# Attention and two gated MLPs on one core: the second MLP's rows 256 to 1279 summed by adding transfers

## The chip, the cores and the metric

The kernel runs on one core of a Trainium2 chip. The metric is the device time of one execution, in microseconds (us). Several executions are timed and their median is given; one more execution is recorded by the hardware profiler.

The engines of the core work beside each other, each through its own list of instructions in order: TensorE (PE, with its weight loads as PEld), VectorE (DVE), ScalarE (ACT), GpSimd (POOL) and SyncE (SP). Transfers between DRAM and on-chip memory are issued from an engine's list and carried out by 16 DMA engines.

## What is computed

Windowed attention gives a matrix x of 2304 tokens by 512; a gated MLP with a sigmoid maps it to another 2304 by 512, and a second gated MLP without the sigmoid maps that to the result:

```python
x = _attn_ref(q, k, v)                    # 4 x 8 heads, window 64, as 2304 x 512
gate = 1.0 / (1.0 + np.exp(-(x @ moe_w_gate)))
x = gate * (x @ moe_w_val) @ moe_w_out    # 512 -> 1536 -> 512
a = x @ moe2_w_a
b = x @ moe2_w_b
return (a * b @ moe2_w_out).astype(np.float32)
```

The MLP weights arrive as 64-bit floats, two 32-bit words each; the kernel rebuilds a 32-bit value from them.

## The kernel before

**Tiling.** The 2304 tokens are nine blocks of 256. The hidden width of 1536 is twelve pieces of 128 (`fc` from 0 to 11, `NF = 12`). Every 32-bit product is made of three TensorE products: each operand is split into a rounded high part and the rest, and high*high, high*low and low*high are summed in PSUM. A tile with an `h` or `l` at its end of the name is such a part.

**Stages.** First come attention and the first MLP of blocks 0 to 4. Then comes the stage that the change is in: the second MLP of the same blocks. Blocks 1 to 4 (tokens 256 to 1279) are taken together as a two by two block product, with seven products instead of eight (`quad`, line 849 for its matmuls, tiles qa, qb, qc). Block 0 is fitted in between by an ordinary product (`hidden`, line 472, tiles gps and vps, and `projection`, line 525, tile acc). After that the last four blocks (tokens 1280 to 2303) go through both MLPs.

**The loop of the stage.** For each `fc` the loop makes the hidden values h of 128 features for the two groups of 512 tokens (tiles hh and hl for one group, h for the other). After every second `fc` (`PAIR = 2`) the output product of these two pieces is put on a list `rest`: 8 jobs, one for each 128 tokens. There are six such pairs, called pair 0 to pair 5 below. A job is one call of `bank_sum`: six matmuls into one PSUM bank (line 987, tile accq, 128 by 512), and then one instruction that empties it. In pair 0 ScalarE copies the bank into the result tile (line 989, tile resf). In pairs 1 to 5 VectorE adds the bank to the result tile (line 991). The result tiles are four of 128 by 2 by 512 that stay on chip through the stage. In pair 5 each job also sends its 128 rows to DRAM from SyncE (line 1122).

**What else runs there.** The weights of the second MLP are decoded in the same stretch, three matrices for each `fc`, up to two pieces ahead. VectorE does the larger part (lines 379 to 401, tiles wi, ex, wa, wb), ScalarE splits and copies (lines 373 to 398), GpSimd makes four sums of weight halves (line 422, tiles s), their low parts (line 430, tiles wq) and one low part (line 401, tile wo). SyncE loads the raw words (tiles st_a, st_b, st_o) and stores the decoded parts in DRAM (tiles ka, kb, ko, kq) for the last blocks. At the end of the stage VectorE and ScalarE also build the operands of the next stage (lines 797, 798 and 805, tiles op and t, from xq), and GpSimd the sums of its first weights (lines 450 and 453, from the loaded tile wf).

**What sets the order.** The program is written in one order, and a scheduler places the instructions on each engine by a simulated timeline. `fill` takes jobs from `rest` and places them between the steps of the next quad; a table `counts` says how many after which step. PSUM has two banks for accq and acc together (`ps_acc`), so the third bank's first matmul waits until the first bank is emptied. The result tiles come from a pool of five buffers (`accp`); the fifth holds block 0's result.

Of the kernel before, what the change touches and what calls it, by code (L numbers as in the profile page):

```python
# [10 lines left out]
F32 = mybir.dt.float32  # L11
# [4 lines left out]
ALU = mybir.AluOpType  # L16
# [5 lines left out]
def tile_window_attention_gated_mlps(ctx, tc, q, k, v, w1g, w1v, w1o, w2a, w2b, w2o, out):  # L22
    nc = tc.nc
# [3 lines left out]
    P = 128  # L27
    NP = H // 2
    NF = DFF // P
    G = 3  # L30
    N = 256
# [3 lines left out]
    W = 2 * N  # L35
# [947 lines left out]
    def bank_sum(dst, pairs, begin):  # L983

        ps = ps_acc.tile([P, W], F32, tag="acc", name="accq")[:, 0:dst.shape[-1]]
        for n, (a, b) in enumerate(pairs):
            nc.tensor.matmul(ps, lhsT=a, rhs=b, start=n == 0, stop=n == len(pairs) - 1)  # L987
        if begin:
            nc.scalar.activation(out=dst, in_=ps, func=AF.Copy)
        else:  # L990
            nc.vector.tensor_tensor(out=dst, in0=ps, in1=dst, op=ALU.add)  # L991
# [114 lines left out]
    def row_banks(res, hs, rows, begin, end):  # L1106


        banks = []
        for i in range(2 * NP):  # L1110
            j, sl = i // NP, slice(i % NP * P, (i % NP + 1) * P)
            cols = (slice(0, CH), slice(CH, W)) if end and rows[0] > N and i == 2 * NP - 1 else (slice(0, W),)
            r0 = rows[j] + i % NP * P
            for c in cols:
                pairs = [(h[j][a][:, sl], o[b][:, c]) for o, h in hs for a, b in ((0, 0), (0, 1), (1, 0))]
                banks.append((pairs, res[i // 2][:, i % 2, c], out[r0:r0 + P, c]))
        for pairs, d, to in banks:

            def job(d=d, p=pairs, b=begin, to=to):
                bank_sum(d, p, b)  # L1120
                if end:
                    nc.sync.dma_start(out=to, in_=d)

            rest.append(job)
        return banks

    x_ops = next(built)
    fill(len(rest))
    x_ops = next(built)
# [15 lines left out]
                    i, at, mybir.DependencyInfo(mybir.DependencyClass.NoSync, mybir.DependencyReason.DATA), reason="paced"  # L1145
                )

    hs, h0s, res = [], [], None
    seconds = (
        lambda: late["hs"].tile([P, 2, W], F32R, tag="hs", name="h1"),  # L1150
        lambda: wts.tile([P, 2, DM], F32R, tag="wa", name="h1"),
# [2 lines left out]
    for fc in range(NF):  # L1154
        alone = ALONE.get(fc, ())
        for i, f0 in enumerate(alone):
            need(NF + f0, NEVER)
            w = parts[NF + f0]
            h0s.append((w, hidden(1, w, x[1, (0,)])))
            fill(2)  # L1160
            if i == len(alone) - 1:
                rest.append(lambda a=(1, 0, h0s, fc == 0, False): projection(*a))
                h0s = []
        need(NF + fc, NEVER)
        if fc == NF - 1:
            eased = len(nc.cur_bb.bb.instructions)
        limit[0] = min(NW - 1, NF + fc + 2)
        if fc == 0:
            res = [accp.tile([P, 2, W], F32, tag="xacc", name=f"resf{i}") for i in range(4)]
        w = parts[NF + fc]  # L1170
        g = [tmp.tile([P, W], F32, tag="hr", name=f"g{i}") for i in range(2)]
        counts = ((0, 0, 1, 1, 1, 1, 0), (0, 0, 1, 1, 1, 1, 0)) if len(rest) <= 4 else ((0, 1, 1, 1, 1, 1, 1), (0, 1, 1, 1, 1, 1, 1))
        extra = max(0, len(rest) - sum(counts[0]))

        def between(i):
            fill(counts[0][i] + (extra if i == 4 else 0))
            for _ in range(((0, 0, 0, 0, 2, 2, 2) if fc == 0 else (1, 1, 1, 0, 1, 1, 1))[i]):
                paced()

        hs.append((w["o"], quad(1, w, x_ops, between, g, seconds[fc % 3], lambda: None)))  # L1180
        if len(hs) == PAIR:
            fill(len(rest))
            row_banks(res, hs, (3 * N, N), fc == PAIR - 1, fc == NF - 1)
            hs = []
    late.clear()
    middle.close()
# [156 lines left out]
```

## Time and profile before

| what | us |
|---|---|
| median of three timed executions | 953.04 |
| lowest and highest of them | 951.15, 953.58 |
| the profiled execution, its own time | 955.45 |
| the profiled execution, span from first to last instruction | 953.5 |
| PE busy within the span | 925.9 |
| DVE, ACT, POOL busy | 708.4, 478.8, 303.3 |

The profiled execution took 955.45 us, of which the span is 953.5; the other 1.95 us lie around it. All times inside the trace count from the start of the span. "Busy" of PE is modelled from pipelined matmuls: six matmuls of 512 columns that wait for nothing follow each other in 1.36 us.

An engine's idle time is put down to the instruction that released it. PE is busy for 97% of the span, so its idle stretches, with their releasers, are where an edit that leaves its matmuls alone can act. The stage of the change lasts from about 375 to 582 us.

### The profile page before, as it was taken

The page shows a single profiled execution, that of the slowest core. Times are in us where ns is not written, and L with a number is a line of the kernel's source. Part 1 is how long each engine was busy: PE and PEld are TensorE (multiplying, and loading weights), DVE is VectorE, ACT ScalarE, POOL GpSimd, SP SyncE. Part 2 cuts the span into 40 slices and gives each one's busy share as a digit, 9 for nine tenths or more (in the row PEclk, how much of TensorE's full clock was granted, in tenths as well). Part 3 has the DMA queues.
Part 4 walks back from the last instruction along what each step waited for, and adds up shares of the span by engine and source line. Part 5 has one row for each costly group of instructions (what it writes and reads, how often), then busy time and mean ns, then how long its engine had stood idle before and what let it go on. Part 6 is the DMA issues. An engine that isn't in the chain of part 4 may idle for free.

```text
span 953.5 us, 15652 instructions
## 1 busy us (share of the span) xinstructions
PE 925.9 (97%) x5504; PEld 773.1 (81%) x5504; DVE 708.4 (74%) x1379; ACT 478.8 (50%) x1063; POOL 303.3 (32%) x321
## 2 busy tenths in 40 slices
PE   7899999999999999999999989999999999999998
PEld 6698888887887788778877777788888888888886
DVE  6998787786569799788999875778788773354445
ACT  7897555686744456564555534655444243211111
POOL 4543222343226714362655336544430000000000
PEclk9999999999999999999999999999999999999999
DMA  8987598988568626565877566354547675554212
GB/s 203 237 237 221 197 326 291 336 286 245 153 220 310 225 109 220 195 220 178 269 236 261 210 198 222 111 188 158 158 150 220 198 275 153 159 173 134 89 66 88
DMA packets 144685, 193.69 MB, mean 203 GB/s; under 512 B 63584, under 2 KB 98912, under 8 KB 143968
## 3 DMA queue, kind: packets, MB, share of 16 engines
q1 hardware_dynamic: 144608, 192.71, 62.5%
q8 instruction: 43, 0.70, 0.3%
q14 instruction: 34, 0.28, 0.1%
HBM read 118.75 MB, written 69.47 MB: 197 GB/s over the span
## 4 chain that ended last, share of the span: by engine, by line
PE 69%; DVE 14%; DMA 5%; POOL 4%; ACT 4%; issue 3%; SPq 0%; DVEq 0%; POOLq 0%; ACTq 0%
PE qa L849 16%; PE accq L987 11%; PE qb L849 8%; PE gps L472 7%; PE vps L472 6%; PE accm L573 6%; PE qc L849 4%; PE accy L950 3%; PE accx L950 2%; DVE ex L392 2%; DVE wi L382 2%; PE xps L228 2%; DVE wi L379 1%; DVE wi L386 1%; DMA st_o<-in_moe_w_out_dram 1%
## 5 line engine op out<-in xcount | busy, mean ns | idle before, releaser
L849 PE MATMUL qa<-op,wq 128*128 128x512 f32 x432 | 112.9, 391 | 2.7 <-ACT r L868 2.3
L849 PE MATMUL qb<-op,wq 128*128 128x512 f32 x432 | 110.7, 390 | 0.9 <-POOL wq L430 0.6
L868 ACT ACTIVATE r<-qa 128x512 f32<-128x512 f32 x108 | 62.5, 594 | 90.0 <-PE qa L849 88.8
L472 PE MATMUL vps<-xh,wb 128*128 128x256 f32 (+1 forms) x392 | 105.6, 338 | 0.2 <-ACT hr L496 0.2
L472 PE MATMUL gps<-xh,wa 128*128 128x256 f32 (+1 forms) x392 | 105.2, 338 | 0.0
L849 PEld LDWEIGHTS qa<-op,wq 128*128 128x128 f32 x432 | 80.9, 188 | 20.4 <-ACT r L868 3.0
L849 PEld LDWEIGHTS qb<-op,wq 128*128 128x128 f32 x432 | 81.0, 188 | 18.4 <-POOL wq L430 1.0
L573 PE MATMUL accm<-hh,wo 128*128 128x512 f32 (+1 forms) x296 | 85.6, 357 | 1.6 <-DVE gacc L550 1.3
L386 POOL TENSOR_TENSOR wi<-wi,low 128x512 int32<-128x512 int32 x36 | 50.1, 1393 | 113.2 <-DVE wi L382 78.3
L472 PEld LDWEIGHTS gps<-xh,wa 128*128 128x128 f32 x392 | 69.2, 191 | 8.5 <-DVE hl L483 0.3
L472 PEld LDWEIGHTS vps<-xh,wb 128*128 128x128 f32 x392 | 69.0, 190 | 8.0 <-ACT hr L496 0.4
L987 PE MATMUL accq<-wo,h 128*128 128x512 f32 (+1 forms) x300 | 71.2, 382 | 3.8 <-DVE resf L991 3.7
L987 PEld LDWEIGHTS accq<-wo,h 128*128 128x128 f32 x300 | 54.8, 188 | 15.8 <-DVE resf L991 4.7
L472 PE MATMUL gps<-xl,wa 128*128 128x256 f32 (+1 forms) x196 | 65.9, 336 | 0.5 <-DVE xl L237 0.5
L472 PE MATMUL vps<-xl,wb 128*128 128x256 f32 (+1 forms) x196 | 65.7, 335 | 0.0
L392 DVE SCALAR_TENSOR_TENSOR ex<-ex,wi 128x512 f32<-128x512 f32 x72 | 53.3, 741 | 14.6 <-ACT ex L376 7.4
L481 ACT ACTIVATE hh<-qa 128x512 fp32r<-128x512 f32 x36 | 21.5, 597 | 84.4 <-DVE qa L881 55.5
L573 PEld LDWEIGHTS accm<-hh,wo 128*128 128x128 f32 x296 | 52.9, 189 | 11.9 <-DVE gacc L550 4.0
L987 PE MATMUL accq<-wo,hh 128*128 128x512 f32 x184 | 56.3, 397 | 1.5 <-ACT hh L481 1.4
L849 PE MATMUL qa<-op,wb 128*128 128x512 f32 x216 | 55.2, 391 | 1.9 <-ACT r L868 1.9
L849 PE MATMUL qc<-op,wa 128*128 128x512 f32 x216 | 56.9, 390 | 0.0
L189 ACT ACTIVATE pr<-pr,stat 128x128 f32<-128x128 f32 x144 | 54.0, 391 | 5.4 <-DVE stat L183 5.2
(180 smaller groups left out, 2154.9 us busy)
## 6 DMA issues: line engine op xcount, KB each, us to landing
wo<-ko SPq DMA_DIRECT2D x27, 512.0 KB, 4.2
wa<-ka SPq DMA_DIRECT2D x27, 512.0 KB, 4.4
st_o<-in_moe_w_out_dram SPq DMA_DIRECT2D x24, 512.0 KB, 5.0
ka<-wa SPq DMA_DIRECT2D x24, 512.0 KB, 5.4
kb<-wb SPq DMA_DIRECT2D x24, 512.0 KB, 3.9
ko<-wo SPq DMA_DIRECT2D x24, 512.0 KB, 5.1
kq<-wq SPq DMA_DIRECT2D x48, 256.0 KB, 4.5
wq<-kq SPq DMA_DIRECT2D x48, 256.0 KB, 3.2
```

The lines of the kernel that those rows point to most:

```text
L189: nc.scalar.activation(out=pr[e][:, j, :], in_=pr[e][:, j, :], func=AF.Exp, bias=nmax[:, e, j:j + 1], scale=-1.0, accum_out=None if t in O ...
L228: nc.tensor.matmul(xps[dims, j, rows], lhsT=vv[:, 2 * j + e, :], rhs=pt[e][:, j, rows], start=True, stop=True)
L382: nc.vector.scalar_tensor_tensor(out=wi, in0=w1, scalar=-(1 << 30), in1=wi, op0=ALU.bitwise_and, op1=ALU.bitwise_or)
L386: (nc.vector if F >= NF else nc.gpsimd).tensor_tensor(out=wi, in0=wi, in1=low, op=ALU.add)
L392: nc.vector.scalar_tensor_tensor(out=wf, in0=wf, scalar=SMALLEST, in1=wi.bitcast(F32), op0=ALU.is_ge, op1=ALU.mult)
L472: nc.tensor.matmul(ps, lhsT=a[:, c * P:(c + 1) * P], rhs=b[:, c, :], start=(n == 0), stop=(n == 3 * NP - 1))
L481: nc.scalar.activation(out=hh, in_=hr, func=AF.Copy, scale=factor)
L573: nc.tensor.matmul(ps[:, m], lhsT=a[:, sl], rhs=b, start=k == 0, stop=k == total - 1)
L849: nc.tensor.matmul(ps, lhsT=a[:, c * P:(c + 1) * P], rhs=b[:, c, :], start=first and n == 0, stop=n == 5, skip_group_check=True,)
L868: nc.scalar.activation(out=r[n], in_=ps, func=AF.Copy)
L950: nc.tensor.matmul(bank[k], lhsT=a[n][i][:, sl], rhs=b[n][j], start=start and m == 0, stop=m == 2, skip_group_check=True,)
L987: nc.tensor.matmul(ps, lhsT=a, rhs=b, start=n == 0, stop=n == len(pairs) - 1)
```

## The change

In the stage of tokens 256 to 1279, every pair's banks are now emptied by ScalarE copies, into tiles called `added` of 128 by 2 by 512 that hold two banks (256 rows) each. A tile is sent to the result in DRAM when both halves are filled: pair 0 by plain stores from SyncE, pairs 1 to 5 by transfers issued from GpSimd that add to what lies in DRAM (`accum_op`). The four result tiles that stayed on chip, and the stores at the end of pair 5, are gone. A tile's send is written two jobs after its second bank (`unsent`), so a pair has nine entries on `rest` instead of eight; the ninth only sends. The manual dependency in `send` keeps the scheduler from placing a transfer ahead of the matmul written before it.

So 40 VectorE adds of a bank become 40 ScalarE copies (48 copies in all, 8 of them were there), and 9 stores of 256 or 128 KB become 4 plain stores and 20 adding transfers of 512 KB. The matmuls stay the same in kind and number.

```diff
+    def added_rows(hs, rows, begin):
+        for i in range(2 * NP):
+            j, sl = i // NP, slice(i % NP * P, (i % NP + 1) * P)
+            pairs = [(h[j][a][:, sl], o[b]) for o, h in hs for a, b in ((0, 0), (0, 1), (1, 0))]
+            r0 = rows[j] + (i % NP - 1) * P
+
+            def job(i=i, p=pairs, to=out[r0:r0 + 2 * P].rearrange("(a p) f -> p a f", p=P) if i % 2 else None):
+                if i % 2 == 0:
+                    added[0] = accp.tile([P, 2, W], F32, tag="xacc", name="added")
+                bank_sum(added[0][:, i % 2], p, True)
+                if i % 2 == 0 and unsent:
+                    unsent.pop()()
+                if i % 2:
+                    unsent.append(lambda t=added[0]: send(t, to, begin))
+
+            rest.append(job)
+        rest.append(lambda: unsent.pop()())
+
+    unsent = []
+
+    def send(t, to, begin):
+        if begin:
+            nc.sync.dma_start(out=to, in_=t)
+        else:
+            at = next(i.name for i in reversed(nc.cur_bb.bb.instructions) if i.engine == mybir.EngineType.PE)
+            since = len(nc.cur_bb.bb.instructions)
+            nc.gpsimd.dma_start(out=to, in_=t, accum_op=ALU.add)
+            for i in nc.cur_bb.bb.instructions[since:]:
+                tc.add_manual_dep(
+                    i, at, mybir.DependencyInfo(mybir.DependencyClass.NoSync, mybir.DependencyReason.DATA), reason="send"
+                )
...
-        if fc == 0:
-            res = [accp.tile([P, 2, W], F32, tag="xacc", name=f"resf{i}") for i in range(4)]
...
-            row_banks(res, hs, (3 * N, N), fc == PAIR - 1, fc == NF - 1)
+            added_rows(hs, (3 * N, N), fc == PAIR - 1)
```

How this moves the instructions is shown at three places at the end of the stage, where pair 5 is emptied. Names are those of the section on the kernel before; a number after a name is a buffer's, and the same tile has another number in the two kernels.

VectorE, before: the adds of pair 5 stand between the steps that build the next stage's operands.

```order
L805 TENSOR_TENSOR t_6901<-xq_6822,t_6863 128x1024
L991 TENSOR_TENSOR resf_4826<-accq,resf_4826 128x512 x2
L798 TENSOR_TENSOR op_6903<-t_6901,op_6903 128x1024
L498 TENSOR_TENSOR vps<-vps,hr 128x256
L991 TENSOR_TENSOR resf_4827<-accq,resf_4827 128x512
L483 SCALAR_TENSOR_TENSOR hl<-vps,hh 128x256
L805 TENSOR_TENSOR t_6939<-xq_6822,xq_6820 128x1024
L991 TENSOR_TENSOR resf_4827<-accq,resf_4827 128x512
L991 TENSOR_TENSOR resf_4828<-accq,resf_4828 128x512
L798 TENSOR_TENSOR op_6941<-t_6939,op_6941 128x1024
```

VectorE, after, the same place:

```order
L805 TENSOR_TENSOR t_6937<-xq_6858,t_6899 128x1024
L798 TENSOR_TENSOR op_6939<-t_6937,op_6939 128x1024
L498 TENSOR_TENSOR vps<-vps,hr 128x256
L483 SCALAR_TENSOR_TENSOR hl<-vps,hh 128x256
L805 TENSOR_TENSOR t_6975<-xq_6858,xq_6856 128x1024
L597 TENSOR_TENSOR xacc_4866<-acc_7088,xacc_4866 128x512
L798 TENSOR_TENSOR op_6977<-t_6975,op_6977 128x1024
```

The adds are gone from VectorE, and the add of block 0's bank (line 597) has moved ahead of the last operand but one.

ScalarE, before, at the same place (line 452 copies the high part of a weight sum, line 797 that of an operand):

```order
L481 ACTIVATE hh<-vps 128x256
L797 ACTIVATE op_6903<-t_6901 128x1024
L452 ACTIVATE wq_7093<-s_7091 128x256
L481 ACTIVATE hh<-vps 128x256
L452 ACTIVATE wq_7098<-s_7096 128x256
L452 ACTIVATE wq_7103<-s_7101 128x256
L797 ACTIVATE op_6941<-t_6939 128x1024
```

ScalarE, after, the same place:

```order
L989 ACTIVATE added<-accq 128x512
L481 ACTIVATE hh<-vps 128x256
L989 ACTIVATE added<-accq 128x512 x2
L797 ACTIVATE op_6939<-t_6937 128x1024
L452 ACTIVATE wq_7120<-s_7118 128x256
L452 ACTIVATE wq_7125<-s_7123 128x256
L989 ACTIVATE added<-accq 128x512
L452 ACTIVATE wq_7130<-s_7128 128x256
L989 ACTIVATE added<-accq 128x512
L481 ACTIVATE hh<-vps 128x256
L797 ACTIVATE op_6977<-t_6975 128x1024
```

The copies of pair 5's last five banks now stand between the weight and the operand copies of the next stage.

GpSimd, after, from the last decoded matrix to the second group of weight sums of the next stage:

```order
L401 TENSOR_TENSOR wo<-ex,wo 128x512
L1155 DMA out_dram<-added 128x2x512 x5
L450 TENSOR_TENSOR s_6988<-wf 128x256
L450 TENSOR_TENSOR s_6993<-s_6988,wf 128x256
L450 TENSOR_TENSOR s_6998<-wf 128x256
L453 TENSOR_TENSOR wq_6990<-s_6988,wq_6990 128x256
L453 TENSOR_TENSOR wq_6995<-s_6993,wq_6995 128x256
L453 TENSOR_TENSOR wq_7000<-s_6998,wq_7000 128x256
L450 TENSOR_TENSOR s_7003<-wf,s_6993 128x256
L453 TENSOR_TENSOR wq_7005<-s_7003,wq_7005 128x256
L1155 DMA out_dram<-added 128x2x512
L450 TENSOR_TENSOR s_7118<-wf 128x256
```

Before, line 450 followed line 401 directly; now the four transfers of pair 4 and the first of pair 5 stand between them, and the other three of pair 5 between the sums. The first twelve, of pairs 1 to 3, stand among lines 422, 430 and 401 in the same way, two for each `fc`.

## Rows read from the trace of the kernel before

**Rows 1.** The page: busy us, share of the span and instructions of each engine.

```profile
PE 925.9 (97%) x5504; PEld 773.1 (81%) x5504; DVE 708.4 (74%) x1379; ACT 478.8 (50%) x1063; POOL 303.3 (32%) x321
```

**Rows 2.** Stretches: length, busy us (instructions) by engine, granted clock, DMA share, GB/s.

```profile
375.00:430.00 55.00, 51.79 (x248) 43.05 (x247) 44.84 (x66) 33.31 (x66) 26.53 (x27) 0.97 0.64 228
430.00:540.00 110.00, 107.98 (x488) 88.29 (x488) 104.88 (x163) 60.35 (x117) 54.08 (x56) 1.00 0.69 231
540.00:582.00 42.00, 37.73 (x202) 31.86 (x201) 31.89 (x43) 14.24 (x25) 14.86 (x16) 1.00 0.55 192
```

**Rows 3.** PE in order of time: start, length, [idle before, its releaser].

```profile
483.09 1.61 PE L849 MATMUL qa<-op,wa 128*128 128x512 f32 x6 [0.58 <-DVE g L871]
...
515.21 0.70 PE L849 MATMUL qb<-op,wq 128*128 128x512 f32 x2 [0.30 <-DVE hl L483]
...
528.27 1.19 PE L987 MATMUL accq<-wo,hh 128*128 128x512 f32 x4 [0.57 <-ACT hh L481]
533.67 1.21 PE L849 MATMUL qb<-op,wq 128*128 128x512 f32 x4 [0.58 <-POOL wq L430]
...
569.85 4.41 PE L987 MATMUL accq<-wo,h 128*128 128x512 f32 x18 [2.48 <-DVE resf L991]
575.45 1.70 PE L987 MATMUL accq<-wo,h 128*128 128x256 f32 x12 [1.20 <-DVE resf L991]
577.55 0.73 PE L525 MATMUL acc<-wo,hh 128*128 128x512 f32 x2 [0.40 <-DVE resf L991]
```

**Rows 4.** DVE by group from 430 to 580: busy, mean ns, idle before.

```profile
L991 DVE TENSOR_TENSOR resf<-accq,resf 128x512 f32<-128x512 f32 (+1 forms) x41 | 26.7, 667 | 2.1 <-PE accq L987 2.0
```

**Rows 5.** Line 989: ns min/median/max, starts; the last list has no entry.

```profile
L989 ACT ACTIVATE resf<-accq x8: 579/598/599, 393.7 to 414.5; 128x512 f32<-128x512 f32 x8
...
who waited for it (us, times):
```

**Rows 6.** DVE in order of time, inside pair 3 and pair 5.

```profile
523.90 0.68 DVE L991 TENSOR_TENSOR resf<-accq,resf 128x512 f32<-128x512 f32 x1
...
569.12 1.27 DVE L991 TENSOR_TENSOR resf<-accq,resf 128x512 f32<-128x512 f32 x2
570.39 1.22 DVE L798 TENSOR_TENSOR op<-t,op 128x1024 fp32r<-128x1024 f32 x1
```

**Rows 7.** ACT by group from 430 to 580: busy, mean ns, idle before, releaser.

```profile
L452 ACT ACTIVATE wq<-s 128x256 fp32r<-128x256 f32 x8 | 3.3, 416 | 12.4 <-POOL s L450 12.2
```

**Rows 8.** ACT in order of time: an operand's high part, and a staged matrix read.

```profile
454.53 0.68 ACT L376 ACTIVATE ex<-st_b 128x512 f32<-128x512 f32 x1 [1.41 <-POOL wo L401]
...
569.23 1.06 ACT L797 ACTIVATE op<-t 128x1024 fp32r<-128x1024 f32 x1 [1.77 <-DVE t L805]
```

**Rows 9.** POOL: line 430 by duration, line 422 by group, and one row in time.

```profile
L430 POOL TENSOR_TENSOR wq<-s,wq x48: 732/1177/1270, 293.8 to 536.6; 128x256 fp32r<-128x256 f32 x48
...
L422 POOL TENSOR_TENSOR s<-ex 128x256 f32<-128x256 f32 x12 | 10.1, 844 | 41.0 <-DVE ex L392 41.0
...
561.41 0.73 POOL L450 TENSOR_TENSOR s<-wf 128x256 f32<-128x256 f32 x1 [21.47 <-DMA wf<-kf]
```

**Rows 10.** Transfers from 430 to 580: count, KB each, median us to landing; one issue on SP.

```profile
ko<-wo SPq DMA_DIRECT2D x7, 512.0 KB, 4.0
ka<-wa SPq DMA_DIRECT2D x6, 512.0 KB, 4.9
...
441.10 0.38 SPq L353 DMA_DIRECT2D st_b<-in_moe_w_b_dram  x1
```

**Rows 11.** DVE in order of time: first and last result tile, pair 4, then pair 5.

```profile
535.29 1.28 DVE L991 TENSOR_TENSOR resf<-accq,resf 128x512 f32<-128x512 f32 x2
...
553.66 0.68 DVE L991 TENSOR_TENSOR resf<-accq,resf 128x512 f32<-128x512 f32 x1
...
560.41 1.28 DVE L991 TENSOR_TENSOR resf<-accq,resf 128x512 f32<-128x512 f32 x2
...
574.72 1.27 DVE L991 TENSOR_TENSOR resf<-accq,resf 128x512 f32<-128x512 f32 x2
```

More of the change, by code (lines that the diff above doesn't have):

```diff
@@ L1125, in row_banks @@
         return banks
+    def added_rows(hs, rows, begin):
[25 more added lines that the diff above has]
+                )
+    added = [None]
     x_ops = next(built)
@@ L1146, in paced @@
                 )
-    hs, h0s, res = [], [], None
+    hs, h0s = [], []
     seconds = (
```

## The prediction

> **What bounds the kernel now.** The first view to read is the busy time of the engines. PE is busy for 925.9 of 953.5 us [rows 1], so at most 27.6 us of the span can go to any edit that leaves the matmuls alone. The second view is the table of stretches, which narrows this to the stage of the change [rows 2]. From 430 to 540 PE is busy for 107.98 of 110 us and DVE for 104.88: PE is the bound and DVE stands right beside it. From 540 to 582, where the operands of the next stage are built, PE is busy for 37.73 of 42 us, and DVE for 31.89. The granted clock is 1.00 in both, that is 2.4 GHz, so no time is hidden in a slow clock there. The stretch ahead of them, 375 to 430, has a clock of 0.97 and idle time too, but pair 0 is emptied by ScalarE in both kernels, so the change hardly touches it.
>
> The third view is PE in order of time with the idle time before each piece [rows 3]. It says which of the 6.3 us of idle time in the two stretches ends on work that the change removes. Three waits at the end of the stage end on the adds themselves: 2.48, 1.20 and 0.40 us, 4.08 together. There PE has filled both banks and stands until DVE, which does a 1.22 us operand step between the adds [rows 6], has emptied one. Four waits before that, 0.58, 0.30, 0.57 and 0.58 us, end on something else (a product's sum, a hidden part, a weight sum), but the chain of each goes back through DVE, which has a run of work with adds in it. The one at 528.27, for instance, follows an add at 523.90 [rows 6] that stood ahead of the decoding and of the hidden product that PE waited for. Together they are 2.03 us. The trace has 6.11 us that the adds cause or lengthen, in seven places.
>
> **The change part by part.** *The adds leave DVE.* 41 adds take 26.7 us, 667 ns each [rows 4]; 26 of them lie within the decoding stretch (24 of pairs 1 to 3, 2 of pair 4), 17.3 us. DVE there comes down from 104.88 to about 87.5 of 110 us. None of this is a gain by itself: 26.7 us of DVE are worth the 6.11 us of PE's idle time and no more, because PE's 107.98 us remain. What is late next at the end of the stage is the operand chain: it loses its adds on DVE as well, and its last step is not needed before the fourth step of the first quad, so I let PE take the whole 4.08.
>
> *The copies go to ACT.* 40 copies of 598 ns are 24 us. ACT is busy for 60.35 of 110 and 14.24 of 42 us [rows 2], so with 26 and 14 of the copies it ends near 69% and 54%. That pair 0 is emptied in this very way and nobody ever waited for it [rows 5] says that the cost can be nothing. Against it speaks the place: in pair 5 the copies stand in ACT's list behind weight copies that wait for GpSimd's sums, 12.2 us of waits over eight of them [rows 7], and behind operand copies of 1.06 us [rows 8]. The lower bound is 0 (not below: an ACT copy can't be earlier than a free DVE would have been), the upper the 4.08 gained there, if ACT takes DVE's part as the late one. One operand copy of 1.06 us and one weight copy of 0.42 ahead of a copy that PE needs make 1.5 us; I take that, since two banks give cover for the rest.
>
> *The stores of pair 0.* Four stores of 512 KB go on SP's list. Behind them stand loads of staged weights; such a load is issued 13.4 us before its data is read (441.10 to 454.53) and its kind lands in about 5 [rows 8, 10]. The 8 us between hide it; without them ACT's decoding would slip by the same amount. Cost 0. The nine stores that go at the end block nothing that PE waits for: 0.
>
> *Twenty adding transfers.* No row shows one. Three things about them can cost time.
>
> The issue on POOL: the trace has SP's issue of a plain transfer at 0.38 us [rows 10] below, and nothing above. I take 1.2, like a GpSimd operation of 1177 ns [rows 9], as it is GpSimd that does it. POOL waits 41.0 us for DVE in six places of line 422 [rows 9], 6.8 us for each `fc`, and two transfers of pairs 1 to 3 fall to each: 3.4 us per issue are free. In pairs 4 and 5, five issues stand in a gap of 21.47 us ahead of the next stage's sums [rows 9]. Cost 0 at up to 3.4 us each. POOL's list also waits at each transfer for the two copies; the sends are written two jobs late, and what stands behind are weight sums for a later `fc`, so 0 again.
>
> The reuse of the tiles: a tile of pair 5 can be filled only when the transfer of pair 4 from the same place has landed. The adds show how long that is: from the end of the second add on the first tile, 536.6, to the first of the next pair, 560.4, 24 us; on the last, 554.3 to 575.3 (the second of the two adds at 574.72), 21 us [rows 11]. With PE some 4 us earlier there, and the issue taken off, about 17 remain. A plain 512 KB store lands in 4.0 to 4.9 us [rows 10]. Cost 0 up to a landing of 17 us. Earlier pairs are further apart: the last adds of pairs 3 and 4 start at 523.90 and 553.66 [rows 6, 11].
>
> The load of the DMA engines: 12 transfers of 0.5 MB in 110 us are 57 GB/s on top of 231, at a share of 0.69 [rows 2]. Counted as plain stores they raise the share by 0.17, to 0.86; counted double, as they also read the result, to 1.03. The first is hidden, the second lets staged loads and the transfers' own landings slide. I take a value nearer the first, since idle gaps of the stretch from 540 (share 0.55) take up what is late.
>
> **A rule that speaks against it.** The Trainium skill, "Collectives: The Full Stack", section "The bandwidth ceiling: the fold count and why AG ≠ RS ≠ AR", says that a transfer that adds reads two sources where a copy reads one, and that its measured rate came to about half. No row of this trace shows it. By it the share would be the 1.03 of the doubled count and a landing, as an estimate, some 8 to 10 us; this would leave the sum as it is and counts for the second rival. The Trainium skill, "SBUF — State Buffer", section "A bandwidth-pool intuition that's wrong (but worth ruling out)", adds that a GpSimd-issued transfer of 620 ns took 3100 when VectorE held the shared port. The trace agrees that GpSimd slows beside VectorE, but by less: line 430 takes 732 ns at best and 1177 at the median [rows 9]. A factor of five on the issue would make 6 us, beyond the 3.4 that are free; that is the third rival.
>
> **The sum.** Seven waits, 6.11 us, less 1.5 for the copies' place on ACT: 4.6 us gained. The profiled execution took 955.45 us (953.5 of span, 1.95 around it), which would become 950.85. It lies 2.4 above the median of the timed runs; against the median of 953.04 the forecast is 948.4 us.
>
> **The rivals.** *ACT becomes the late one at the end.* At the end of the stage ACT's list holds copies of pair 5 behind weight copies, which wait for GpSimd, which waits for the load of wf; so a bank is free only after a load has landed. For it: the 12.2 us of waits [rows 7] and the load at 561.41 that GpSimd waited for [rows 9]. Against it: two banks of cover and the early pair 0 [rows 5]. Then the 4.08 us stay, and with the copies ahead of products in the decoding stretch also part of the 2.03: a gain of 0 to 2.8 us, 950.2 to 953, at 951.5. This case also takes in that the change doesn't do what it says, because ACT's waits put the hidden parts as late as DVE did.
>
> *Slower by the landing of the adding transfers.* The place is pair 5, whose four tiles wait for pair 4's transfers. Each us of landing beyond 17 is a us of PE, once, because all four are late by the same. It is slower than before from a landing of 22 us on; at 26 us the time is 948.4 + 9 = 957. For it: the doubled share of 1.03, and five transfers that stand in a row on GpSimd's list. Against it: plain stores land in under 5 us beside the same loads [rows 10].
>
> *Slower by the issue on GpSimd.* Beyond 3.4 us per issue, each `fc` of pairs 1 to 3 puts its weight sums off by two times the excess. That such a delay reaches PE is seen at 533.67, where PE waited 0.58 us for line 430 [rows 3]. At 4.2 us per issue, 0.8 times 12 issues are 9.6 us: 958. It decides from about 3.8 us on.
>
> **How the numbers follow.** About 0.3% of the time, 2.9 us, is what a measurement of this kernel can tell from no change: faster means below 950.2, slower above 955.9. The forecast, with 946 to 950 around it, gets 0.54; a larger gain, by decoding that runs ahead and shifts later work, 0.02; the first rival 0.24; landing 0.12; issue 0.08. That is faster 0.56, same 0.24, slower 0.20. The range goes from 945, which is the whole 6.11 and 2 us of later work, up to 957, where about half of the two slower cases lie inside.
>
> **What would show it.** In the changed kernel's trace PE's waits at accq at the end of the stage should be gone or under 1.5 us in total, and the last product of block 0 end some 4 us earlier after the same start. DVE should be busy for about 87.5 of the 110 us after pair 0, ACT for some 76. The page should show a second DMA queue with 20 transfers and a landing under 17 us. Copies that wait for a transfer in pair 5 show the second rival; line 430 late with PE behind it the third; waits of PE for line 989 the first. If PE's idle time from 430 to 582 doesn't fall at all, the reading of the DVE chain was wrong.

## The result, and the profile after

The changed kernel takes 962.45 us (median of four runs, 960.20 to 964.91), the kernel before 952.62 beside it. The ratio is 1.0105, with a 95% interval of 1.0074 to 1.0136. The change makes the kernel slower by 1.0%, against a forecast of 948.4 and a range of 945 to 957. The profiled execution took 964.91 us, 963.1 of them span, 9.6 more than before. Its stretches of time (length, busy us by engine, granted clock, DMA share, GB/s), the first two of which answer to [rows 2], and two short ones:

```profile
430.00:540.00 110.00, 101.67 (x448) 81.99 (x447) 96.03 (x132) 68.38 (x134) 66.99 (x67) 0.98 0.97 274
540.00:582.00 42.00, 38.19 (x198) 32.30 (x197) 17.34 (x22) 18.47 (x34) 14.99 (x15) 0.98 0.87 216
...
535.00:540.00 5.00, 5.00 (x16) 3.93 (x16) 3.68 (x6) 2.31 (x5) 3.91 (x5) 0.66 0.71 275
580.00:585.00 5.00, 5.00 (x17) 3.93 (x16) 3.27 (x4) 3.15 (x7) 4.92 (x6) 0.66 0.85 150
```

PE's busy time from 430 to 540 fell from 107.98 to 101.67 us: it idles more. VectorE came down, but to 96.03 instead of the forecast 87.5, although 26 adds of 0.67 us left that stretch. ScalarE was busy for 68.38 us of it, where some 76 had been forecast. The DMA share rose from 0.69 to 0.97, GpSimd's busy time from 54.08 to 66.99. One detail of the change: before, the last bank of pair 5 went in two halves of 256 columns (the 12 matmuls at 575.45 in [rows 3]), after in one. So 41 adds became 40 copies, and PE has 5498 matmuls in place of 5504.

To find the 9.6 us, take the same two steps of PE in both kernels: a product in pair 0 and one in the first step of the next stage. Before (start, length, idle time before and its releaser):

```profile
380.12 1.65 PE L849 MATMUL qa<-op,wb 128*128 128x512 f32 x6 [0.53 <-ACT r L868]
386.39 1.96 PE L849 MATMUL qa<-op,wq 128*128 128x512 f32 x6 [1.89 <-ACT r L868]
...
589.44 1.65 PE L849 MATMUL qa<-op,wb 128*128 128x512 f32 x6 [0.69 <-ACT r L868]
```

After, with the larger waits between:

```profile
378.38 1.67 PE L849 MATMUL qa<-op,wb 128*128 128x512 f32 x6 [0.54 <-ACT r L868]
384.64 2.14 PE L849 MATMUL qa<-op,wq 128*128 128x512 f32 x6 [1.84 <-ACT r L868]
...
460.43 0.73 PE L987 MATMUL accq<-wo,hh 128*128 128x512 f32 x2 [1.45 <-DVE xacc L597]
462.77 0.73 PE L987 MATMUL accq<-wo,hh 128*128 128x512 f32 x2 [1.38 <-DVE xacc L597]
520.28 1.66 PE L987 MATMUL accq<-wo,h 128*128 128x512 f32 x6 [0.91 <-ACT added L989]
...
534.75 2.06 PE L849 MATMUL qa<-op,wq 128*128 128x512 f32 x6 [3.74 <-ACT r L868]
...
579.38 5.99 PE L987 MATMUL accq<-wo,h 128*128 128x512 f32 x18 [3.59 <-ACT added L989]
...
597.27 0.96 PE L849 MATMUL qa<-op,wb 128*128 128x512 f32 x3 [0.69 <-ACT r L868]
```

From the first to the last it is 209.32 us before and 218.89 after: all of the loss lies here. The waits of 0.2 us and more between them sum to 9.68 before and 15.22 after, 5.5 more. The rest is mostly the clock. Behind each of the two waits over 3.5 us PE ran a slice of 5 us at a mean granted clock of 0.66, so most of it at 1.2 instead of 2.4 GHz; a third such slice, from 385, follows the 1.84. Each costs 5 times 0.34, 1.7 us, so 5.1 in all, against 1.7 in the same stretch before, behind a wait of 1.89. The seven waits of [rows 3] are gone, and others stand in their place.

The transfers (busy us, mean ns, idle before; then KB and median us from issue to landing):

```profile
L1155 POOL DMA_DIRECT2D out_dram<-added x20 | 24.5, 1223 | 46.3 <-ACT added L989 41.5 <-ACT wq L427 4.7
```

```profile
out_dram<-added POOLq DMA_DIRECT2D x20, 512.0 KB, 7.1
...
st_b<-in_moe_w_b_dram SPq DMA_DIRECT2D x5, 512.0 KB, 7.3
```

An issue holds GpSimd for 1.2 us, as forecast, and lands in 7.1. But GpSimd stands 41.5 us at the transfers for ScalarE's copies, and other transfers land later (st_b in 7.3 us, before in 5.0). And one VectorE instruction, line 382 of the decoding, took 3.47 us, and two more of that line 2.70 and 2.35; no VectorE instruction of the stage took 2 us before. GpSimd and VectorE in order of time at the longest:

```profile
444.50 1.36 POOL L1155 DMA_DIRECT2D out_dram<-added  x1 [0.30 <-ACT added L989]
445.57 3.12 POOL L430 TENSOR_TENSOR wq<-s,wq 128x256 fp32r<-128x256 f32 x4
...
445.78 3.47 DVE L382 SCALAR_TENSOR_TENSOR wi<-st_o,wi 128x512 int32<-128x512 int32 x1
```

It starts inside the issue and ends half a microsecond after the last of the four weight sums behind the issue.

At the end of the stage, the chain of the 3.59 us wait begins with the load of wf and passes GpSimd's sums and ScalarE's list:

```profile
565.43 0.32 SPq L830 DMA_DIRECT2D wf<-kf  x1
...
572.42 0.73 POOL L450 TENSOR_TENSOR s<-wf 128x256 f32<-128x256 f32 x1 [6.32 <-DMA wf<-kf]
...
573.18 0.42 ACT L452 ACTIVATE wq<-s 128x256 fp32r<-128x256 f32 x1 [5.92 <-POOL s L450]
573.51 0.58 ACT L989 ACTIVATE added<-accq 128x512 f32<-128x512 f32 x1
...
578.43 0.42 ACT L452 ACTIVATE wq<-s 128x256 fp32r<-128x256 f32 x1 [2.10 <-POOL s L450]
578.75 0.58 ACT L989 ACTIVATE added<-accq 128x512 f32<-128x512 f32 x1
```

Bank copies stand behind weight copies that wait for GpSimd. These are the mechanism and the place of the first rival.

### The profile page after: what moved, and what is told of

Its sections match the earlier page's. It is cut to its first block, busy times and chain, and to the rows that moved or that the text cites. A ratio compares the mean times of both kernels' runs of the same rounds, so it can differ in the third digit from the quotient of the medians.

```text
span 963.1 us, 15689 instructions
## 1 busy us (share of the span) xinstructions
PE 929.9 (97%) x5498; PEld 774.9 (80%) x5498; DVE 696.2 (72%) x1338; ACT 497.9 (52%) x1103; POOL 329.2 (34%) x341
## 4 chain that ended last, share of the span: by engine, by line
PE 69%; DVE 13%; DMA 5%; ACT 4%; POOL 4%; issue 3%; SPq 0%; DVEq 0%; POOLq 0%; ACTq 0%
PE qa L849 16%; PE accq L987 12%; PE qb L849 8%; PE gps L472 7%; PE vps L472 6%; PE accm L573 6%; PE qc L849 3%; PE accy L950 3%; PE accx L950 2%; DVE ex L392 2%; DVE wi L382 2%; PE xps L228 2%; DVE wi L379 1%; PE sps L170 1%; DVE wi L386 1%
```

## The experiments

All times are medians; the ratio is to the kernel before on the same chip.

### Which part of the transfer costs

Theories: GpSimd's list (issue and waits there), traffic, or ScalarE's list and the new order of work. Four edits of `send`:

```diff
 e1_no_send        -        else:
                   +        elif False:
 e2_sync_plain     -        if begin:
                   +        if True:
 e3_pool_plain     -            nc.gpsimd.dma_start(out=to, in_=t, accum_op=ALU.add)
                   +            nc.gpsimd.dma_start(out=to, in_=t)
 e5_small_add      +            nc.gpsimd.dma_start(out=to[0:8], in_=t[0:8], accum_op=ALU.add)
```

> The ScalarE copies stay, the 20 adding transfers of pairs 1 to 5 are left out (their sums never reach the result; only pair 0 is stored). Three theories of why the changed kernel took 962.5 instead of 948.4. GpSimd's list: the issues (1.20 us each) and their waits for ScalarE's copies (up to 4.7 us) hold up the weight sums that stand behind them; then this kernel gets all of it back, 949 to 953, and VectorE's longest instruction of line 382 falls from 3.47 to about 1.6. Traffic: the DMA engines at 0.97 instead of 0.69 make the loads late; then also 949 to 953, with landings back at 4 to 5 us. ScalarE's list and the order at the end: copies stand behind split copies that wait; then 957 to 962, with the TensorE wait of 3.6 us at the end still there. So this run tells the third from the first two.

> The 20 transfers are plain stores from SyncE instead of adding transfers from GpSimd (only the last pair stays in the result, the sums are left out): 10 MB are written as before, nothing is read, and GpSimd's list has neither issues nor waits. GpSimd's list: 949 to 953, near the kernel without transfers. Traffic: the write half of it is still there, so half of what the kernel without transfers gains, about 956, DMA share about 0.87 in the window of the stage. ScalarE's list: as the kernel without transfers, 957 to 962.

> The same 20 transfers from GpSimd at the same places, but without the adding (they overwrite; the sums are left out): the order on every engine is that of the changed kernel, only the reading of the old rows is gone. GpSimd's list: no change, 961 to 963. Traffic: about 956 to 958 and a DMA share of about 0.87. ScalarE's list: 961 to 963.

> The same 20 adding transfers at the same places, but each of only 8 of the 128 partitions (32 KB instead of 512 KB; most of the sums are left out). Issue and wait on GpSimd stay, the traffic is nearly gone. GpSimd's list: 960 to 963 (if an issue of fewer packets is also shorter, a few us less). Traffic: as without transfers, 949 to 953. ScalarE's list: 957 to 962.

Then the two halves of GpSimd's part, at the same places:

```diff
 e6_wait_only      +            nc.gpsimd.tensor_copy(out=t[:, 0, 0:2], in_=t[:, 1, 0:2])
 e7_issue_only     +            ready = x[1, (0,)][0].bitcast(F32).rearrange("p (a k) n -> p a (k n)", a=2)
                   +            nc.gpsimd.dma_start(out=to, in_=ready, accum_op=ALU.add)
 e8_small_issue_only +          nc.gpsimd.dma_start(out=to[0:8], in_=ready[0:8], accum_op=ALU.add)
```

> In the place of each of the 20 adding transfers GpSimd copies two elements per partition inside the same tile, which waits for the same ScalarE copies but issues nothing (the sums are left out). The runs so far put some 8 us on GpSimd's list (962.3 with small transfers, 954.1 without any); this run and the next tell its two parts apart. If the wait is the cost (the weight sums stand behind a copy that comes late): 960 to 963. If the issue is (1.20 us of GpSimd each, and VectorE's line 382 beside it up to 3.47 us): 954 to 956.

> The 20 adding transfers stay in their places at full size, but take their data from a tile that was complete long before (so the sums are wrong and the copied banks go nowhere): GpSimd issues without waiting for ScalarE. If the wait is the cost: 954 to 956. If the issue is: 960 to 963.

> The changed kernel with 20 adding transfers of 8 partitions from a tile that was complete long before (the sums are wrong, the copied banks go nowhere): GpSimd's issue alone, with neither the wait nor the traffic. The wait alone was 956.2, the issue with full traffic 962.4. If the issue itself costs the 6 to 8 us: 959 to 963, with VectorE's line 382 stretched to 2 us and more. If it costs only together with the wait or with the traffic: 954 to 956.

| run | issue on GpSimd | wait for copies there | traffic | us | ratio, 95% |
|---|---|---|---|---|---|
| e1 | no | no | no | 954.06 | 1.0002 to 1.0030 |
| e2 | no | no | writes | 954.65 | 1.0018 to 1.0043 |
| e6 | no | yes | no | 956.23 | 1.0026 to 1.0057 |
| e8 | yes | no | small | 956.05 | 1.0016 to 1.0042 |
| e5 | yes | yes | small | 962.32 | 1.0067 to 1.0145 |
| e7 | yes | no | adds | 962.41 | 1.0075 to 1.0114 |
| e3 | yes | yes | writes | 962.13 | 1.0058 to 1.0120 |
| after | yes | yes | adds | 962.45 | 1.0074 to 1.0136 |

VectorE's list is the same in all eight, instruction for instruction (in e2 but for two), so the runs compare the transfers and not another order of the work there.

Three things follow. First, even without a transfer the ScalarE copies bring nothing: 954.06, not 948.4. No theory had put e1 or e2 between 953 and 956. Second, against e1 each part alone costs some 2 us or less, but the issue together with either of the others costs 8. Two cases were not run: the wait with traffic but without an issue, and the traffic of adds without an issue; so in e7 that traffic alone may be the cost. e6 and e7 came out near the theory that the issue is the price (e7 inside its 960 to 963, e6 0.2 us above its 954 to 956); e8, with the issue and little traffic, shows that by itself it is not. Third, the reading half of the add is not needed for a loss of this size (e3; its five runs lie between 957.6 and 964.0, and its trace is of one at 957.6).

Why the copies bring nothing is seen in PE's waits of e1 from 430 to 582, which are all there are over 0.2 us:

```profile
458.72 0.72 PE L987 MATMUL accq<-wo,hh 128*128 128x512 f32 x2 [1.37 <-DVE xacc L597]
...
515.19 1.65 PE L987 MATMUL accq<-wo,h 128*128 128x512 f32 x6 [0.63 <-ACT added L989]
520.43 0.73 PE L987 MATMUL accq<-wo,hh 128*128 128x512 f32 x2 [0.64 <-ACT added L989]
528.50 2.47 PE L849 MATMUL qa<-op,wq 128*128 128x512 f32 x6 [2.99 <-ACT r L868]
570.49 4.37 PE L987 MATMUL accq<-wo,h 128*128 128x512 f32 x18 [1.46 <-ACT added L989]
```

They sum to 7.09 us, in place of the 6.11 of [rows 3]. The largest ends on ScalarE, whose list has the copy that PE needs behind weight copies that wait for GpSimd, the last of them here:

```profile
526.99 0.42 ACT L427 ACTIVATE wq<-s 128x256 fp32r<-128x256 f32 x1 [0.72 <-POOL s L422]
...
527.88 0.57 ACT L868 ACTIVATE r<-qa 128x512 f32<-128x512 f32 x1
```

Behind it a stretch at the low clock costs 1.7 us more (granted clock 0.91 from 525 to 530 and 0.75 from 530 to 535).

### Why issue and wait cost more together

e5 and e6 have the same order and the same wait; one issues, the other copies two elements. In e5, at one group of weight sums:

```profile
519.40 0.86 POOL L1155 DMA_DIRECT2D out_dram<-added  x1 [4.71 <-ACT added L989]
520.01 3.08 POOL L430 TENSOR_TENSOR wq<-s,wq 128x256 fp32r<-128x256 f32 x4
...
519.55 4.10 DVE L382 SCALAR_TENSOR_TENSOR wi<-st_a,wi 128x512 int32<-128x512 int32 x1
...
526.76 0.73 PE L987 MATMUL accq<-wo,hh 128*128 128x512 f32 x2 [2.99 <-ACT added L989]
```

In e6, the same place:

```profile
516.85 0.40 POOL L1155 COPY added<-added 128x2 f32<-128x2 f32 x1 [4.47 <-ACT added L989]
517.21 4.19 POOL L430 TENSOR_TENSOR wq<-s,wq 128x256 fp32r<-128x256 f32 x4
...
517.24 1.25 DVE L382 SCALAR_TENSOR_TENSOR wi<-st_a,wi 128x512 int32<-128x512 int32 x1
```

Beside the same four sums, line 382 takes 1.25 us in e6 and 4.10 in e5. In e6 the engines take turns: a sum takes 1.05 us, and VectorE's next instructions are stretched a little. In e5 the sums run through at 0.77 each, and VectorE stands until they are over. The wait does its part by place: while GpSimd waits at a transfer, the sums behind it become ready, so that the issue has a run of work right behind it. In e8, without the wait, the issue is done while GpSimd has nothing else to do, and only one VectorE instruction takes over 2 us; in e5 four do, in e1 and e6 none.

Not every such place does it. In the changed kernel the same instruction starts inside the issue, with the same four sums behind it, and the engines take turns as in e6:

```profile
520.53 1.21 POOL L1155 DMA_DIRECT2D out_dram<-added  x1 [4.71 <-ACT added L989]
521.31 4.37 POOL L430 TENSOR_TENSOR wq<-s,wq 128x256 fp32r<-128x256 f32 x4
...
520.68 1.24 DVE L382 SCALAR_TENSOR_TENSOR wi<-st_a,wi 128x512 int32<-128x512 int32 x1
```

So it is at 484.79 (1.24 us, for 4.09 at the same place in e5). What decides between the two was not found. That VectorE and GpSimd meet at a shared port fits the Trainium skill, "SBUF — State Buffer", section "Who interferes with whom": an instruction of VectorE with two inputs in SBUF contends with one of GpSimd that reads SBUF. Line 379, with a single input, was held too (4.87 us in e9 below, 3.58 in f1), which this sentence does not cover. That an issue can let the whole run go first is what these rows show.

In the changed kernel this is one part of the loss. Between the same two steps of PE as above, e1 takes 209.84 us and the changed kernel 218.89, with waits of 10.53 and 15.22 in all, and with one and three stretches at the low clock that cost 1.7 us each. Of the 4.7 us of waits, 1.5 stand around 460 (1.45 and 1.38, for 1.37 in e1), where VectorE has hardly paused since its 3.47 us, and 0.75 at the product's copy at 534.75, with the 2.35 us of line 382 ahead of it. The largest part, 2.1, is at 579.38, behind the load of wf, which landed after 6.9 us, in e1 after 3.2.

Two runs put 20 small issues into the kernel before: one after every second bank of pairs 1 to 5, or two behind each low part of wo, where GpSimd has mostly nothing ready. The program is otherwise kept, but the scheduler also moves other work. Up to 480 us VectorE's and GpSimd's lists in e9 are those of the kernel before; behind that some 30 VectorE instructions stand elsewhere, and in e11 more.

```diff
 e9_before_small_issue, in row_banks, after every second bank of pairs 1 to 5
+                        nc.gpsimd.dma_start(out=spares[0][len(sent) % 16 * 8:][:8], in_=ready[len(sent) % 16 * 8:][:8], accum_op=ALU.add)
...
 e11_before_issue_after_group, in decode_pair, after line 401
+            for k in range(2):
+                nc.gpsimd.dma_start(out=spares[0][to], in_=ready[to], accum_op=ALU.add)
...
```

> The kernel before, with its VectorE adds and everything else kept, and beside that 20 small adding transfers of 8 partitions, issued by GpSimd in pairs 1 to 5 from a complete tile into a spare buffer in DRAM: the issue added to the kernel before and nothing else. If an issue costs because it stands among the weight sums and beside VectorE's two-input instructions: 955 to 960. If GpSimd's idle time hides it, as forecast: 952.5 to 953.5.

> As the kernel before with 20 small issues (966.0), but two issues each stand directly behind the low part of wo (line 401), where GpSimd has no weight sum to do for some microseconds, instead of in the middle of the sums. If an issue costs only where a run of GpSimd work follows it at once (VectorE's instruction that starts beside the issue then ends with the run, 5.25 us in the run before): 953 to 956, and no VectorE instruction over 2.4 us beside an issue. If the issue itself costs, wherever it stands: 962 to 968.

e9: 965.99 us, ratio 1.0113 to 1.0155. e11: 954.63, 0.9998 to 1.0030. The issues cost 13 us at one place, more than any theory had, and some 2, not told from none, at the other. e9, at a place ahead of 480:

```profile
475.50 0.74 POOL L422 TENSOR_TENSOR s<-ex 128x256 f32<-128x256 f32 x1 [6.56 <-DVE ex L392]
476.19 0.76 POOL L1132 DMA_DIRECT2D spare<-xh  x1
...
478.84 2.29 POOL L430 TENSOR_TENSOR wq<-s,wq 128x256 fp32r<-128x256 f32 x3
...
476.44 5.25 DVE L401 TENSOR_TENSOR wb<-ex,wb 128x512 fp32r<-128x512 f32 x1
...
482.95 2.93 PE L849 MATMUL qa<-op,wa 128*128 128x512 f32 x6 [3.13 <-DVE g L871]
```

VectorE's subtraction starts in the issue and ends at 481.69, 0.56 us after GpSimd's run; the adds of g stand behind it, and PE waits 3.13 us. Two more such places (4.87 us of VectorE at 532.01, 4.15 at 576.76) stand ahead of PE waits of 4.70 and 3.34. In e11 (line 412 is the issue, lines 438 and 446 the sums) no VectorE instruction in the stage takes over 1.8 us:

```profile
489.36 1.51 POOL L401 TENSOR_TENSOR wo<-ex,wo 128x512 fp32r<-128x512 f32 x1 [6.70 <-ACT wo L398]
490.82 1.59 POOL L412 DMA_DIRECT2D spare<-xh  x2
493.50 0.74 POOL L438 TENSOR_TENSOR s<-ex 128x256 f32<-128x256 f32 x1 [1.09 <-DVE ex L392]
```

This is no clean comparison of the place alone: the order differs, e11's issues lie between 372 and 539 us and e9's between 428 and 582, and at two of e11's places (413 and 452) four sums do stand right behind. There the VectorE instruction beside the issue took 1.04 and 1.01 us, so a run of ready work behind an issue is not enough by itself.

### Whose copy it is

```diff
 e4_vector_copy (and e10, with elif False in send)
+        elif fresh:
+            nc.vector.tensor_copy(out=dst, in_=ps)
...
```

> The banks of pairs 1 to 5 are copied by VectorE instead of ScalarE into the same tiles, with the same adding transfers; nothing is left out. If ScalarE's list is what holds the banks (copies behind split copies that wait), this gains over the changed kernel: 955 to 959. If GpSimd's issues cost the time whoever copies: 961 to 965. If VectorE is the engine at its limit, slower than the changed kernel: over 965.

> As the run before, but the 20 adding transfers are left out (the sums of pairs 1 to 5 reach no result). With ScalarE's copies this was 954.1. If the place of the copy does not matter: 953 to 955. If ScalarE's list is what eats the gain of the copies: 950 to 952. The difference to the run before is the price of the transfers with VectorE's copies; the same 8 us as with ScalarE's, by the theory of the issues.

e10: 953.88 us, ratio 0.9992 to 1.0016; e4: 969.57, 1.0149 to 1.0183. Without transfers the place of the copy does not matter. With them VectorE's copies lose 16 us, where the theory of the issues had 8, and are 7 us slower than ScalarE's. How much of the 7 is the relief of VectorE is not shown, for the largest wait of e4 is another way in which transfers cost:

```profile
558.65 1.06 ACT L797 ACTIVATE op<-xq 128x1024 fp32r<-128x1024 f32 x1 [10.48 <-DMA xq<-bx]
...
560.25 2.93 PE L849 MATMUL qa<-op,wb 128*128 128x512 f32 x6 [8.90 <-ACT r L868]
```

ScalarE waits for a load of the next stage's operands (3.38 us at the same place in e10), and the copy r that PE needs stands behind it.

### Moving the transfers

```diff
 f1_later_send     +                if i % 2 == 0 and len(unsent) > 1:
                   +                    unsent.pop(0)()
                   ...
 f3_send_after_group, in decode_pair, after line 401
                   +            while unsent:
                   +                unsent.pop(0)()
                   ...
 f4_two_after_group   the same with  for _ in range(min(2, len(unsent)))
 e12_after_group_small  as f3, with to[0:8] and t[0:8]
```

> The changed kernel with each tile sent two jobs later (two tiles unsent instead of one), so that the copies are further ahead when GpSimd comes to the transfer; nothing is left out. If the wait is the cost: 955 to 958. If the issue is: 961 to 963. Either way not faster than the kernel before, since without any transfer it was 954.1.

> The changed kernel with its full adding transfers, each sent directly behind the low part of wo (line 401) and only the last five among the sums of the next stage; nothing is left out. If the place of the issue is the cause: 954 to 958, against 962.4 of the changed kernel and 969.4 of the one that sent each tile later. If the issue or the traffic costs wherever it stands: 961 to 966. Not under 952 by any theory, since without transfers it was 954.1.

> The kernel that sends directly behind the low part of wo (968.9), with each transfer of only 8 of the 128 partitions (32 KB; most of the sums are left out). There VectorE had no long instruction beside an issue, but three or four transfers of 512 KB stood in a row, the four loads of xq landed after 11.9 us instead of 5.2, and ScalarE waited 7.5 us for them with bank copies behind it. If these bursts of traffic are the second cause: 954 to 957, xq landings at 4 to 6 us. If it is the issues or the new order of the work: 963 to 969.

> The same kernel with full transfers, but at most two in a row behind each low part of wo; nothing is left out. If bursts are the second cause, part of the loss goes: 957 to 964. If the traffic of the adds costs however it is spread, or the order does: 965 to 970. Not under 954 by any theory.

| run | us | ratio, 95% |
|---|---|---|
| f1 | 969.39 | 1.0150 to 1.0193 |
| f3 | 968.85 | 1.0151 to 1.0190 |
| f4 | 964.35 | 1.0115 to 1.0160 |
| e12 | 960.88 | 1.0080 to 1.0117 |

f1 and f3 lie 6.4 and 2.9 us above the upper range that was expected, and 11 above the one that moving was to reach. f3 has one VectorE instruction over 2 us before 580 (2.20 at 455.36, beside an issue), but three and more transfers in a row (lines are numbered 10 higher there: 807 is the operand copy, 999 the bank copy):

```profile
555.36 1.06 ACT L807 ACTIVATE op<-xq 128x1024 fp32r<-128x1024 f32 x1 [3.75 <-DMA xq<-bx]
556.32 0.58 ACT L999 ACTIVATE added<-accq 128x512 f32<-128x512 f32 x1
...
556.95 2.92 PE L997 MATMUL accq<-wo,h 128*128 128x512 f32 x6 [3.64 <-ACT added L999]
```

The four loads of xq land there in 11.9 us at the median, in e1 in 5.2. Taking the traffic away gives 7 to 8 us back (e12; xq lands in 6.7), spreading it 3 to 4.5 (f4), with intervals that still touch. But in f4 xq still lands in 11.3 us, so what came back there came from something else. Waits for xq are also in f1 (7.6 us) and e7 (4.3, with PE behind for 4.25), so loads that land late beside the transfers are a second way to lose. e12 and f4 lie between the ranges that were expected. e12 still loses some 9 us to the kernel before: three issues in a row at 449.38 run on into sums that are ready, with a VectorE instruction of 2.54 us beside them, and PE waits 3.07 us at 466.12 and 3.42 at 532.52. How much of this is the issues and how much the order of the work, which differs between f3, f4 and e12, was not told apart.

### Only where the gain was expected

```diff
 f2_last_pair
...
+            if fc < NF - 1:
+                row_banks(res, hs, (3 * N, N), fc == PAIR - 1, fc == NF - 1 - PAIR)
+            else:
+                added_rows(hs, (3 * N, N), False)
```

> Pairs 0 to 4 as before (summed on chip by VectorE, stored after pair 4 by SyncE), and only pair 5 by ScalarE copies and 4 adding transfers; nothing is left out. Before, the three TensorE waits at the end were 4.08 us; without transfers the copies left 1.46 there. If the end alone is worth that: 949.5 to 951. If the four issues and the late weights of the next stage take it back: 952 to 955.

954.03 us, ratio 1.0006 to 1.0028: no gain. At the end, PE's 4.08 us at the adds became 2.38, the larger part of it:

```profile
565.01 4.24 PE L987 MATMUL accq<-wo,h 128*128 128x512 f32 x12 [2.11 <-ACT added L989]
```

and four issues stand between the sums of line 450, with VectorE's line 805 at up to 2.74 us beside them. No version here beats the kernel before.

## Why the prediction was wrong

**The bound** was read rightly: PE's idle time in the stage decides, and the loss lies there.

**The gain of 4.6 us** failed at the term for the copies' place on ScalarE. It took 1.5 of a possible 4.08, on the ground that two banks cover the rest. e1, which has nothing but the copies, shows 7.09 us of new waits for 6.11 removed, 1.7 us of slow clock, and 954.06 us. The upper bound was too low as well: it counted bank copies at the end, but the largest new wait (2.99) is that of a product's copy r in the middle of the stage, behind a weight copy. The first rival's words (weight copies that wait for GpSimd, with ScalarE as the late one) describe what happened; its 951.5 is 2.6 us below e1. Its gain of up to 2.8 does not follow from its own terms: with the 4.08 kept, 2.03 is the most that is left.

**VectorE's relief** was sized at 17.3 us; it came to 8.9, since lines 382, 386 and 392 grew by 8.0 us together. That this relief is worth nothing by itself agrees with e1 and e10: VectorE is busy for 91.98 and 104.36 us of the 110 there, and the times are 954.06 and 953.88.

**The issue at no cost** is the step that turned the sign. Its price, 1.2 us, was exact. But the sum set it against GpSimd's idle time per `fc`, 6.8 us, as if only its length counted. The length is not all: right ahead of ready sums it can stop VectorE for 2.3 to 5.3 us. What the sum had at 0 measured 2 us for the issue alone (e8 against e1) and 8 us with the wait or the traffic (e5, e7). The third rival named the engine and a delay of weight sums, but let it decide only from 3.8 us per issue. It was wrong in the threshold, and in the victim: VectorE's decoding was stretched beside an issue that itself stayed at 1.2 us. The Trainium skill, "SBUF — State Buffer", section "A bandwidth-pool intuition that's wrong (but worth ruling out)", has its factor of five on the time of a transfer; the prediction put it on the issue. There it did not show: 1.20 us at the median and 1.42 at most. The slowdown fell on VectorE.

**The waits at the transfers** were also put at 0, since what is behind them is for a later `fc`. GpSimd stood 41.5 us there. Alone that costs 2 us (e6), but in e5 it is what sets an issue right ahead of ready sums.

**Landing** (7.1 us at the median, 10.9 at most, for 17 allowed) was right, and tiles were free in time: the second rival did not occur in the changed kernel (in f3 two copies waited 1.24 and 1.61 us for a landing). **The share**, 0.97, lies inside the bounds of 0.86 to 1.03, but near the doubled end and not the one taken. Of the rule of the Trainium skill, "Collectives: The Full Stack", section "The bandwidth ceiling: the fold count and why AG ≠ RS ≠ AR", which is given there for collectives and by which a landing was estimated at 8 to 10 us, the trace shows 7.1 and that share. And the loads that became late (wf here, xq in f3, e4 and e7) have ScalarE and its bank copies behind them, which the sum left out.

**The clock** was no term at all. The two waits of 3.74 and 3.59 us brought 1.7 us each of slow matmuls behind them, so each cost 5.3 to 5.4.

## What to carry to other kernels

Idle time of an engine need not hide a new instruction, even if its sum is large: look at the place, at what is queued ready behind it, and at what a neighbouring engine does there. A move of work from a busy to an idle engine is priced by what stands ahead of it in the new engine's list, and by what that work waits for. Costs that slack hides one at a time need not be hidden together: price them in pairs.

## What the hardware showed that was not expected

- A GpSimd transfer issue of 0.76 to 1.36 us with a run of GpSimd work right behind it can hold a VectorE instruction until the run is over: 3.47, 4.10 and 5.25 us, for 0.69 alone and 1.25 beside the same sums without an issue. At other such places the engines took turns (1.24 us twice in the changed kernel). It struck instructions with two on-chip inputs (lines 382, 401, 805), and also line 379 with a single one (4.87 us in e9, 3.58 in f1). What holds VectorE was not looked into further.
- An adding transfer of 512 KB from on-chip memory to DRAM landed in 5.6 to 10.9 us, beside a DMA share of 0.97; its issue took 1.20 us of GpSimd, that of a plain one 0.73, that of an adding one of 32 KB 0.86.
- Behind each of two PE waits of 3.6 and 3.7 us stood a slice of 5 us at a mean granted clock of 0.66, with PE busy all through it. So it was behind a wait of 1.84 us in the same trace, but behind the one of 2.48 in the kernel before the clock stayed at 1.00.
